# A causal convolution and a SwiGLU layer on one core: the second pair's tokens fetched by thirds, three of its sums moved

## The chip, the cores and the metric

The program runs on one core of a Trainium2 chip. Its engines are named as in the profile: PE multiplies matrices, DVE and POOL work on vectors, ACT evaluates functions, SP issues DMA transfers. The metric is the device time of one execution in microseconds. The kernel before took 2605.76 us, the median of four runs (2605.2 to 2605.84).

## The reference

The input `x` has 8 sequences of 4096 tokens with 192 channels. The first part is a causal convolution of seven taps: the 192 channels are eight heads of 24, each head has its own seven weights (a softmax over the taps), and a token is the weighted sum of itself and the six tokens before it. The second part works on all 32768 tokens: each is scaled by the inverse root of the mean of its squares, then

```
g   = xn @ w_gate        # 192 -> 1536
val = xn @ w_val         # 192 -> 1536
out = (silu(g) * val) @ w_out   # 1536 -> 192
```

Everything is float32.

## The kernel before, in words

The tokens are taken in 32 pairs of blocks: a pair is 1024 tokens, two halves g of T = 512. For each pair DVE, ACT and POOL make the convolution and the scaling (`yn`, heads on partitions), the heads are written to a scratch tensor `xd` of 192 channels by 1024 tokens in DRAM (`place`, L636, one transfer of 16 partitions for each head of 24 channels), and it is read back with the channels on partitions into `xb` (`fetch`, L649 for pair 1; `fetch_part`, L662, for the later pairs). `xb` is [128, 2, 3, 512]: the lower 64 partitions and the upper 64 hold the same tokens, the second index is the half g, the third the third k of the channels (64 channels each). `x_op(i)` names such pieces: 0 to 2 are the three thirds of half 0, 3 to 5 those of half 1, 6 to 15 are ten sums in `xc`.

Pair 0 goes through a plain path: `plain` multiplies by the weights (L1012), and `outer` multiplies by `w_out` (L1052) and sums the two row halves of each output bank (ACT copies one half, L1060; DVE adds the other, L1064; one store for each half of the tokens, L1069). From pair 1 on a product scheme is used that needs fewer multiplications, on combinations of the inputs: eleven token sums for a pair (`x_sum`, L671, listed in `XSUM`), combinations of the weights (`w_sums`, L346 and L350, made once by POOL) and of `w_out` (`out_sums`, L826, made once by POOL). PE's products for a pair (L760) run in the order of `CHAINS`; a product (v, i) goes into the bank of its sum v, once for the lower row half (h = 0) and once for the upper (h = 1). The chain of pair 1 begins with (4,11), (1,4), (5,6), (4,9), (0,8). Each product is two records in the trace.

The order of the work around the change is set by a list with a place for each action: `put(at, action)` enters it, `emit` gives it out by rising place. The outer stage starts at `base`, one of its 96 steps is 37.5 places, and `c` is `base + 200`. Each engine and each DMA queue executes its share in this order. While PE works through the outer products of pair 0, the list holds:

- on POOL the weight sums of the last two units (L350, L346), then for pair 2 the factor of the scaling (L478, L481, L484), one L826, the scaling itself (L499, which waits for the transpose L491 on DVE), and the eleven other L826;
- on SP the writes of heads 0, 2, 4, 6 of pair 1 (the odd heads are on ACT's queue), then `fetch(1)`, the store of pair 0's first half (L1069), pair 2's heads, the store of the second half, and loads of later tokens;
- on DVE taps of pair 2 (L445), L1064 for the first bank of pair 0, pair 2's reduction (L472, L473, L474), the first two token sums of pair 1, L1064 for the second bank (ps6), nine more sums, the transpose L491, L1064 for the third bank (ps7) and for the fourth (ps4). Then comes the work of pair 1.

PE's product (1,4) puts its upper half into bank ps7, and (5,6) into ps4, which the L1064 set free. The sums are given out in the order 0, 1, 7, 2, 3, 5, 6, 10, 8, 9, 4 of `XSUM`. Sum 0 reads the middle thirds of both halves, sum 1 the last third and sum 0's result. Product (4,11) reads what sum 6 writes, (1,4) what sum 10 writes, (5,6) the middle third of half 1 itself, (0,8) sum 8's result.

After pair 1 the order is written out by hand in `ORDER`, the same for each pair, and `fetch_part` reads the tokens by halves.

Of the kernel before, what the change touches and what calls it, by code (L numbers as in the profile page):

```python
# [19 lines left out]
def kernel(  # L20
# [22 lines left out]
    T = 512  # L43
# [3 lines left out]
    HP = P // 2  # L47
    KP = D // HP
# [188 lines left out]
    def load_out(i):  # L237
# [28 lines left out]
        out=taps[:], in0=w_sb[:], in1=stat[:].to_broadcast([P, H, K]), op=ALU.subtract  # L266
# [7 lines left out]
        out=taps[:], in0=taps[:], in1=ssum[:].to_broadcast([P, H, K]), op=ALU.mult  # L274
# [51 lines left out]
    xb = cst.tile([P, 2, KP, T], F32, name="xb")  # L326
# [315 lines left out]
    def fetch(p):  # L642

        if p >= PAIRS:
            return
        xd = scr.pop(p)
        for g in (1, 0):
            for rows in (LOW, UPP):
                nc.sync.dma_start(  # L649
                    out=xb[rows, g],  # L650
                    in_=xd[:, g * T : (g + 1) * T].rearrange("(k p) t -> p k t", p=HP),
                )

    mark = dram.tile([1, 2], F32, name="mark")
# [343 lines left out]
    def plain(hts):  # L998


        groups = [(u, g, f) for u in range(NU) for g in (1, 0) for f in range(NF)]
        groups[0 : 2 * NF] = [(0, g, f) for f in range(NF) for g in (1, 0)]
        held = {}

        def products():
            for u, g, f in groups:
                if len(hts) <= u:
                    hts.append(big.tile([P, 2, NF, T], F32, name="ht"))
                bks = held[u, g, f] = [free[h].pop(0) for h in range(2)]
                for k in range(KP):  # L1010
                    for h in range(2):
                        nc.tensor.matmul(  # L1012
                            out=bank(h, bks[h])[:], lhsT=wf[u][HALF[h], k * NF + f, :],
                            rhs=xb[HALF[h], g, k, :], start=(k == 0), stop=(k == KP - 1),
                            skip_group_check=True,
                        )
                yield

        def silus():
            for i in groups:  # L1020
                sg = tiles.pop(0)
                nc.scalar.activation(out=sg[:], in_=bank(0, held[i][0])[:], func=AF.Silu)
                held[i].append(sg)
                yield

        def values():
            for u, g, f in groups:
                *bks, sg = held.pop((u, g, f))
                nc.vector.tensor_tensor(  # L1029
                    out=hts[u][:, g, f, :], in0=bank(1, bks[1])[:], in1=sg[:], op=ALU.mult  # L1030
                )
                tiles.append(sg)
                for h in range(2):
                    free[h].append(bks[h])
                yield

        return products(), silus(), values()
# [117 lines left out]
    p, sl, v = plain(hts)  # L1155
# [25 lines left out]
    base = NU * SPAN  # L1181
    put(base - 1, lambda: outer(0, hts, base))
    put(base + 445, functools.partial(next, pieces["t"], None))
    put(base + 450, functools.partial(fetch, 1))
    both.extend(flat[:, i * T : (i + 1) * T] for i in range(NK - len(both)))
    rest.extend(t[:, 2, :] for t in tl6)
    put(base + 1317, lambda: tiles.extend(t[:, i, :] for t in tl6 for i in range(2)))
    c = base + 200
# [11 lines left out]
    later(norm(2), c + 1510, c + 1600, c + 2310, c + 2420, c + 2440)  # L1200
    later(place(2), c + 2450)
    xat = [c + i for i in (1660, 1730, 2060, 2130, 2200, 2270, 2290)]
    xat += [c + i for i in (2360, 2370, 2380, 2390)]
    for i, at in zip((0, 1, 7, 2, 3, 5, 6, 10, 8, 9, 4), xat):
        put(at, functools.partial(x_sum, i))
    later(out_sums(), *[base + 2600 + 60 * i for i in range(4 * NM)])
# [49 lines left out]
```

## Time and profile before

| what | value |
|---|---|
| median of four runs | 2605.76 us |
| the profiled execution | 2605.84 us |
| its span, first to last instruction | 2603.7 us |
| PE busy, share of the span | 2571.3 us, 99% |
| DVE, POOL, ACT | 2308.9 us (89%), 2188.5 us (84%), 1545.5 us (59%) |
| mean granted clock of PE | 0.998 |
| pair 0: plain products, outer products | 38.3 to 100.9 us, 101.0 to 134.3 us |
| heads of pair 1 written, fetch of pair 1 issued | from 112.6 us, 119.2 to 121.8 us |
| eleven sums of pair 1 on DVE | 129.8 to 137.8 us |
| first product of pair 1 | 135.40 us |

A line of a timeline has the start in us, the length, the engine, the line of the kernel, the operation, what it writes and reads, shapes and a count, and in brackets the idle time of the engine before it and what ended it. A group line has, behind the bar, busy time, mean ns of one, then the idle time before the group. Instructions that follow each other without a wait overlap by up to 0.1 us in the records, so the length of one is a little more than its share of the engine. PE's upper and lower row halves work at the same time.

### The profile page before, as it was taken

The numbers are of one execution on the slowest core, as the hardware profiler recorded it, in microseconds if no ns is written. First come the engines' busy times: TensorE is split into PE (matmuls) and PEld (weight loads), VectorE is DVE, ScalarE is ACT, GpSimd is POOL, SyncE is SP. The second block draws the span as 40 slices with busy tenths as digits, with TensorE's granted clock in tenths as the row PEclk, the third lists the DMA queues.
The fourth block names the chain that finished last, engine by engine and source line by source line (L and its number), as shares of the span: only waits on it lengthen the run. The fifth ranks groups of instructions, "written<-read, shape, count | busy, mean of one in ns | idle before, by whom it ended". The sixth has DMA issues, their size and how long they took to land.

```text
span 2603.7 us, 60625 instructions
## 1 busy us (share of the span) xinstructions
PE 2571.3 (99%) x23794; PEld 1766.3 (68%) x23794; DVE 2308.9 (89%) x3679; ACT 1545.5 (59%) x2812; POOL 2188.5 (84%) x1786
## 2 busy tenths in 40 slices
PE   6999999999999999999999999999999999999999
PEld 3776667666676667776676676666766666766666
DVE  8998989989989889889899898899898898988975
ACT  5375555765556765557655567655576555676554
POOL 3888889888898888898888898888988888988877
PEclk9999999999999999999999999999999999999999
DMA  6222331313322223312133222233222333122210
GB/s 144 51 51 45 63 61 39 58 33 63 63 51 44 45 51 63 63 39 56 32 63 64 51 44 45 50 63 63 41 53 38 58 63 56 40 54 41 50 44 13
DMA packets 512602, 137.35 MB, mean 53 GB/s; under 512 B 484284, under 2 KB 486844, under 8 KB 512189
## 3 DMA queue, kind: packets, MB, share of 16 engines
q1 hardware_dynamic: 509068, 132.80, 27.1%
q8 instruction: 186, 3.05, 0.5%
q10 hardware_dynamic: 3248, 0.69, 0.1%
q14 instruction: 100, 0.82, 0.1%
HBM read 83.87 MB, written 49.55 MB: 51 GB/s over the span
## 4 chain that ended last, share of the span: by engine, by line
PE 95%; DVE 2%; DMA 1%; issue 0%; ACT 0%; POOL 0%; SPq 0%; ACTq 0%; DVEq 0%; POOLq 0%
PE ps L760 62%; PE ps L900 33%; PE ps L1012 1%; DVE ht L1029 0%; DMA x<-in_x_dram 0%; DMA xb<-xd 0%; DVE xc L304 0%; DVE y L406 0%; DVE y L421 0%; DVE xc L671 0%; DVE y L394 0%; PE ps L595 0%; DVE wf L319 0%; ACT xb L615 0%; DMA xd<-yn 0%
## 5 line engine op out<-in xcount | busy, mean ns | idle before, releaser
L760 PE MATMUL ps<-xc,wf 64*128 64x512 f32 x4960 | 1217.6, 591 | 2.2 <-DVE xc L671 1.1
L760 PEld LDWEIGHTS ps<-xc,wf 64*128 64x128 f32 x4960 | 684.4, 186 | 375.7 <-issue 179.2
L760 PE MATMUL ps<-xb,wf 64*128 64x512 f32 x2480 | 683.1, 591 | 0.0
L709 ACT ACTIVATE tile<-ps 128x512 f32<-128x512 f32 x678 | 391.2, 593 | 391.1 <-PE ps L760 297.6
L709 ACT ACTIVATE tls<-ps 128x512 f32<-128x512 f32 (+1 forms) x562 | 323.3, 589 | 438.0 <-PE ps L760 221.3
L812 POOL TENSOR_TENSOR ht<-ht,tile 128x512 f32<-128x512 f32 x329 | 419.0, 1275 | 142.8 <-ACT tile L805 66.2
L760 PEld LDWEIGHTS ps<-xb,wf 64*128 64x128 f32 x2480 | 356.3, 187 | 180.5 <-issue 94.1
L812 POOL TENSOR_TENSOR ht<-ht,tls 128x512 f32<-128x512 f32 x260 | 330.6, 1274 | 85.9 <-ACT tls L805 42.5
L709 ACT ACTIVATE ps<-ps 128x512 f32<-128x512 f32 (+1 forms) x589 | 336.1, 580 | 89.1 <-PE ps L760 31.8
L928 POOL TENSOR_TENSOR early<-ht 128x512 f32<-128x512 f32 x279 | 354.9, 1277 | 4.9
L445 DVE SCALAR_TENSOR_TENSOR ps<-xh,tp,ps 128x512 f32<-128x512 f32 x450 | 320.2, 748 | 2.7 <-ACT ps L437 0.5
L900 PE MATMUL ps<-ht,wo_sb 128*32 128x128 f32 (+2 forms) x5208 | 318.6, 380 | 0.0
L900 PEld LDWEIGHTS ps<-ht,wo_sb 128*32 128x32 f32 x5208 | 234.1, 110 | 81.7 <-POOL ht L812 23.6
L900 PE MATMUL ps<-ht,x 128*32 128x128 f32 (+2 forms) x4464 | 250.7, 379 | 0.0
L792 DVE TENSOR_TENSOR tile<-ps,tile 128x512 f32<-128x512 f32 x349 | 237.4, 683 | 10.6 <-PE ps L760 5.6
L928 POOL TENSOR_TENSOR ht<-ht 128x512 f32<-128x512 f32 x186 | 238.9, 1285 | 4.9
L792 DVE TENSOR_TENSOR ht<-ps,tile 128x512 f32<-128x512 f32 x328 | 222.5, 680 | 6.2 <-ACT tile L709 6.2
L900 PEld LDWEIGHTS ps<-ht,x 128*32 128x32 f32 x4464 | 184.9, 110 | 60.8
L805 ACT ACTIVATE tile<-tile 128x512 f32<-128x512 f32 x349 | 214.5, 625 | 0.1
L792 DVE TENSOR_TENSOR ht<-ps,tls 128x512 f32<-128x512 f32 x292 | 198.9, 681 | 7.2 <-ACT tls L709 3.6
L792 DVE TENSOR_TENSOR tls<-ps,tls 128x512 f32<-128x512 f32 x271 | 184.8, 683 | 16.6 <-PE ps L760 13.4
L900 PE MATMUL ps<-early,x 128*32 128x256 f32 (+2 forms) x3348 | 196.0, 379 | 0.0
(130 smaller groups left out, 3249.2 us busy)
## 6 DMA issues: line engine op xcount, KB each, us to landing
xb<-xd SPq DMA_DIRECT2D x124, 384.0 KB
xd<-yn SPq DMA_DIRECT2D x244, 96.0 KB
xh<-in_x_dram SPq DMA_DIRECT2D x192, 105.0 KB
out_dram<-o_sb SPq DMA_DIRECT2D x122, 96.0 KB
out_dram<-o_sb SPq DMA_DIRECT2D x62, 128.0 KB
xh<-in_x_dram SPq DMA_DIRECT2D x56, 98.4 KB
out_dram<-o_sb SPq DMA_DIRECT2D x122, 32.0 KB
ht<-in_moe_w_gate_dram SPq DMA_DIRECT2D x12, 192.0 KB
```

Of the source, the lines that this page charges most:

```text
L445: nc.vector.scalar_tensor_tensor(out=dst, in0=xk, scalar=w, in1=at, op0=ALU.mult, op1=ALU.add)
L709: nc.scalar.activation(out=dst, in_=src, func=AF.Copy, scale=float(s))
L760: nc.tensor.matmul(out=self.new(v, h, True) if first else self.old(v, h), lhsT=wf[self.u][HALF[h], WAT[i], :], rhs=x_op(XOP[i])[HALF[h]], ...
L792: nc.vector.tensor_tensor(out=self.hv(v) if h else t[:], in0=self.old(v, h), in1=t[:], op=plus(s))
L805: nc.scalar.activation(out=t[:], in_=src[:], func=AF.Silu)
L812: engine[eng].tensor_tensor(out=self.hv(v), in0=src, in1=t[:], op=ALU.mult)
L900: nc.tensor.matmul(out=self.bank(b)[i * Q : (i + 1) * Q, at : at + n], lhsT=left, rhs=cols, start=fresh, stop=True, skip_group_check=True, ...
L928: engine[eng].tensor_tensor(out=dst, in0=a, in1=b, op=op)
L1012: nc.tensor.matmul(out=bank(h, bks[h])[:], lhsT=wf[u][HALF[h], k * NF + f, :], rhs=xb[HALF[h], g, k, :], start=(k == 0), stop=(k == KP - 1 ...
```

## The change

`fetch(1)` reads `xd` by the thirds of the channels in place of the halves of the tokens. There are six transfers where there were four; each covers 64 channels and all 1024 tokens, so that it depends on the writes of only those heads that its 64 channels touch (heads 0 to 2, 2 to 5, and 5 to 7). The bytes are the same. In the list, the places of the last three sums (8, 9 and 4) go from `c + 2370`, `2380`, `2390` to `base + 2895`, `2900`, `2905`, which is behind L491 and the L1064 of ps7 and ahead of the L1064 of ps4. The first eight sums keep their order. On PE and ACT the order of the instructions is as before; on POOL as well.

```diff
@@ fetch(p)
-        for g in (1, 0):
+        for k in range(KP):
             for rows in (LOW, UPP):
                 nc.sync.dma_start(
-                    out=xb[rows, g],
-                    in_=xd[:, g * T : (g + 1) * T].rearrange("(k p) t -> p k t", p=HP),
+                    out=xb[rows, :, k, :],
+                    in_=xd[k * HP : (k + 1) * HP, :].rearrange("p (g t) -> p g t", t=T),
                 )
@@ the list for pair 1
     xat = [c + i for i in (1660, 1730, 2060, 2130, 2200, 2270, 2290)]
-    xat += [c + i for i in (2360, 2370, 2380, 2390)]
+    xat += [c + 2360] + [base + i for i in (2895, 2900, 2905)]
     for i, at in zip((0, 1, 7, 2, 3, 5, 6, 10, 8, 9, 4), xat):
         put(at, functools.partial(x_sum, i))
```

## The prediction

> **What bounds the kernel now.** I read the page's busy table first, then the groups by line, then the chain of waits around the second pair's fetch (112 to 139 us), and there the timelines of PE, DVE and POOL.
>
> ```profile
> PE 2571.3 (99%) x23794; PEld 1766.3 (68%) x23794; DVE 2308.9 (89%) x3679; ACT 1545.5 (59%) x2812; POOL 2188.5 (84%) x1786
> ...
> L760 PE MATMUL ps<-xc,wf 64*128 64x512 f32 x4960 | 1217.6, 591 | 2.2 <-DVE xc L671 1.1
> ```
>
> PE is the bound. Of the large matmul groups (L760, L900) this one alone has idle time before it, 2.2 us in the whole run. PE's timeline shows that both pieces lie at the start of pair 1, which is what the edit touches:
>
> ```profile
> 135.40 1.95 PE L760 MATMUL ps<-xc,wf 64*128 64x512 f32 x6 [1.11 <-DVE xc L671]
> 138.44 0.69 PE L760 MATMUL ps<-xc,wf 64*128 64x512 f32 x1 [1.08 <-DVE o_sb L1064]
> ```
>
> Nothing later waits, so what the edit gains or loses here reaches the end unchanged, and the gain has a ceiling. PE's last outer matmul (L1052) ends at 134.29; three f32 products of two records each run at 0.43 us a record on each row half. The first product without a gap after it is the upper half of (5,6), in PE's order the third on that half. It starts at 139.40 in the records; without any wait it could start after two products, four records, at 134.35 + 4 x 0.43 = 136.1. So the edit can win 3.3 us at most. The chain of waits (start, length, what) says what holds it:
>
> ```profile
> 115.25 3.81 DMA xd<-yn
> ...
> 121.18 8.53 DMA xb<-xd
> ...
> 135.90 1.89 DVE xc L671 x3
> 137.78 0.15 DVE s L491
> 137.94 0.45 DVE o_sb L1064
> ```
>
> The heads land until 119.06, the fetch until 129.71, then eleven sums and the L1064 that frees bank ps7. The next rows to read are POOL's and DVE's in steady work, near 205 us, since the two share something:
>
> ```profile
> 204.68 1.74 POOL L928 TENSOR_TENSOR tls<-ht,nt 128x512 f32<-128x512 f32 x1
> ```
>
> ```profile
> 205.20 1.77 DVE L671 TENSOR_TENSOR xc<-xb 128x512 f32<-128x512 f32 x1
> ```
>
> And POOL's timeline at the place itself:
>
> ```profile
> 125.00 3.41 POOL L350 TENSOR_TENSOR wf<-wf 128x128 f32<-128x128 f32 x7
> 128.38 1.02 POOL L346 TENSOR_SCALAR wf<-wf 128x128 f32<-128x128 f32 x2
> 129.47 0.20 POOL L478 TENSOR_SCALAR r<-r 128x8 f32<-128x8 f32 x1
> 129.75 1.68 POOL L481 TENSOR_TENSOR r<-r,nhalf 128x8 f32<-128x8 f32 x1
> ...
> 138.07 2.87 POOL L499 TENSOR_TENSOR yn<-y,s 128x1536 f32<-128x1536 f32 x1 [4.69 <-ACT tile L709]
> ```
>
> A token sum (L671) takes 0.69 alone and 1.77 beside a POOL tensor_tensor, and POOL's op takes 1.74 where the page's mean for L928 is 1.28: they take turns, instruction by instruction. Beside L481 a sum keeps its 0.69, and an L1064, which reads PSUM, keeps 0.45 to 0.55 beside L499. Before the change the sums start at 129.83, when POOL has just finished its weight sums (129.40), and L499 waits for L491 (its wait ends at 137.98, 0.04 after L491), behind the last sum. So today they hardly meet.
>
> **The change, part by part.**
>
> *Issues on SP.* Four L649 of 0.60 to 0.64 us become six: two more, 0.5 us (an L659 costs 0.26) to 1.7 us (an L144 0.86); I take 1.3. They are hidden. By the landing records the heads arrive at 115.1, 115.6, 116.7, 117.1, 117.8, 118.1, 118.9 and 119.1. SP is free at 116.07, so the first third (heads 0 to 2) issues at 116.8, the second (to head 5) at 118.2, the third at 119.5 to 120.8. Next on SP is the L1069 store at 131.7, which waits for DVE.
>
> *Landing.* The same 1.57 MB. Before: issue 119.18, first packet 120.6, last landing 129.71, 9.1 us of flow. After: first packet about 118.3, last landing near 127.4, the second third near 124.7. Bounds: no gain (129.7), or 3 us.
>
> *The first sums move under POOL's weight sums.* DVE is free from 125.57 (L474). Sum 0 needs only the middle third and goes at once; sum 1 needs the last, about 127.6. From 125.41 POOL needs 4.26 us of its own to the end of L478 (129.67). Five sums get turns in it, 0.62 each: 3.1, so L478 ends at 132.8. L481 follows, 1.68, to 134.5; the two L484 (0.2 each) after sum 10's rest, to 135.05. DVE's eight sums are through by 134.7 (before: 135.98), so they win 1.3, not 2.3.
>
> *The three sums behind L1064.* New DVE order: sum 10, L491, L1064 (ps7), sums 8, 9, 4, L1064 (ps4). L491 waits for L484 and ends at 135.4, ps7 is free at 135.9. But L491 also releases POOL's L499, which starts about 135.65, after an L826, while DVE is in L1064. Sum 8 then stands behind L499: 135.65 + 2.87 = 138.5. After it sums and the eleven queued L826 take turns: 3 x 0.58 + 2 x 0.55 = 2.85, to 141.4, and L1064 0.53, to 141.9. The same reckoning puts the L1064 of before at 139.20, where the trace has 138.85, so I take 0.35 off: 141.55. The matmul follows 0.12 later, at 141.7 against 139.40: **+2.3 us**. PE's order is unchanged, so it stands at bank ps4 with only two and a half products done. Bounds: if POOL's chain kept its time (L499 from 132.9), -0.4; if a sum lost to L499 only the 1.1 us that the 1.77 row shows, 1.8 less, +0.5; if all eight sums took turns ahead of it and nothing is taken off, +3.9.
>
> What waits behind: L786 and the rest of DVE wait for PE as before, ACT too; POOL's next L812 at 148 has slack, since the L826 end near 146; the stores and loads on SP come 2 to 4 us later, and the next fetch is at 189.
>
> The Trainium skill has a rule for this (SBUF — State Buffer, "Who interferes with whom"): a VectorE instruction with two SBUF inputs and a GpSimd instruction that reads SBUF exclude each other for the whole instruction. The rows agree for 1.28 us instructions; none shows a sum against the 2.87 us of L499. By the rule the step costs the full +2.3 above; by the shortest reading of the row, the +0.5.
>
> *PE's clock.* The three sums open a silence on PE from about 137.0 (products (4,11), (1,4) and the lower half of (5,6) done) to 141.7, 4.7 us. PE's timeline has one like it, and the view by stretches (PE busy first, PEclk third from the end) shows the clock around it:
>
> ```profile
> 29.62 0.80 PE L595 MATMUL ps<-xc,y 128*128 128x128 f32 x2 [5.59 <-ACT xc L588]
> ```
>
> ```profile
> 20.00:30.00 10.00, 3.48 (x9) 1.25 (x7) 9.12 (x16) 7.68 (x23) 0.00 (x0) 0.84 1.17 178
> 30.00:40.00 10.00, 8.90 (x55) 7.98 (x56) 8.75 (x23) 8.16 (x17) 0.00 (x0) 0.82 0.23 25
> ...
> 134.00:138.00 4.00, 2.24 (x8) 0.70 (x6) 3.96 (x8) 1.08 (x2) 0.00 (x0) 1.00 0.00 0
> ```
>
> PEclk 0.84 and 0.82 over 10 us each are 3.2 + 3.6 = 6.8 us at half clock (26.83 to 33.66 in the clock records), 4.0 of them with work waiting: 2.0 us lost. Gaps of 1.1 us (134 to 138) left the clock at 1.00. A silence of 4.7 us is much nearer to 5.59: **+2.0 us**. Bounds: 0, and half of 6.8, 3.4.
>
> The skill (TensorE: Matmul & The Clock Gate, "What's actually happening") lets the clock fall after one idle window of about 3.4 us, free-running. A window of it that is wholly idle falls inside 4.7 us only about four times in ten (an estimate from that page), and then the sum would more often be +2.3 alone. The drop in the trace came 2.8 us after the last matmul, sooner than that.
>
> **Sum.** 2.3 + 2.0 = +4.3 on the profiled execution's own 2605.84 (span 2603.7 and 2.1 around it) is 2610.1; that execution is 0.08 above the median, so 2610.0.
>
> **Rivals.** *Slower without the clock drop:* +2.3, 2608.1. For it: the products just before the silence may keep the clock up, and whether it falls may hang on its phase. *As meant:* if L499 did not hold up sums 8, 9, 4 nor the weight sums the first ones, L1064 (ps4) ends near 135.3 and PE runs through: -3.3, 2602.5. Against it: the 1.77 rows. *Nearly even:* L499 early (133) or the sums passing it, -0.4 to +0.5, about 2605.8. *Past the bound:* the place is again L1064 (ps4); POOL's chain a further 0.6 late (+2.9) and the clock down from the resumption on for its longest, 3.4 of loss: +6.3, 2612.1. It decides once the loss of clock exceeds 2.9 on top of 2.3. That the change does not do what it says is excluded by the order of both programs: six L649 with waits on their own heads, three L671 moved.
>
> **How the numbers follow.** Chances: +4.3 case 0.48 (2608.2 to 2611.6), no clock drop 0.24 (2606.3 to 2609), even 0.10, as meant 0.10, past the bound 0.08. Leaving out the last two, the range is 2604.5 to 2611.6. A change under 0.2% (5.2 us) is what a measurement of this kernel can hardly tell from none: 2600.5 to 2611.0. Over it lie the last case and a fifth of the first: slower 0.17. Faster by more than 3.3 is excluded by the ceiling, but for surprises: 0.01. Same 0.82.
>
> **What would show it.** L671's first start at 125.6 to 126, in records over 1 us beside L350; L478 at 132 to 133; an L671 of over 2 us beside L499; the L1064 of ps4 ending near 141.5; PE idle over 4 us before (5,6), released by L1064; PEclk under 1.00 in 138 to 146. I am wrong if sum 8 runs 0.69 beside L499, if L499 starts before 134, or if PE's idle stays under 3 us.

## The result and the profile after

The changed kernel takes 2609.55 us, the median of 41 runs (2608.18 to 2611.42), against 2605.78 us for the kernel before in the same comparison (61 runs). The ratio is 1.0014, with a 95% interval of 1.001 to 1.0019: slower by 0.14%, 3.8 us, inside the 0.2% that was called no change, and on the slow side of it. The profiled execution took 2610.75 us, its span 2608.6.

On the page the idle time of PE's products has moved from one group to another, from 2.2 us in two pieces to 4.4 us in one:

```profile
PE 2575.3 (99%) x23794; PEld 1764.1 (68%) x23794; DVE 2315.6 (89%) x3679; ACT 1545.6 (59%) x2812; POOL 2191.4 (84%) x1786
...
L760 PE MATMUL ps<-xb,wf 64*128 64x512 f32 x2480 | 682.3, 591 | 4.4 <-DVE o_sb L1064 4.4
```

PE's timeline shows the place. PE as a whole now has no idle time up to the lower half of (5,6); only the upper half of (1,4) is held for about 0.4 us, to 136.05, by the L1064 of ps7, while other products run. The upper half of (5,6) stands for 4.38 us until L1064 has freed ps4. Such a stretch in which PE runs no matmul is called a silence here.

```profile
136.66 0.59 PE L760 MATMUL ps<-xb,wf 64*128 64x512 f32 x1
141.62 1.22 PE L760 MATMUL ps<-xb,wf 64*128 64x512 f32 x1 [4.38 <-DVE o_sb L1064]
141.63 1.22 PE L760 MATMUL ps<-xc,wf 64*128 64x512 f32 x1
142.64 1.06 PE L760 MATMUL ps<-xb,wf 64*128 64x512 f32 x1
```

What stands before that L1064 is in DVE's timeline. The first token sum starts at 126.18, 3.65 us earlier than before, and sum 10 ends at 133.04. Then DVE waits 2.26 us for POOL, and after L491 and the L1064 of ps7 the last three sums take 5.2 us:

```profile
126.18 0.93 DVE L671 TENSOR_TENSOR xc<-xb 128x512 f32<-128x512 f32 x1
...
132.35 0.69 DVE L671 TENSOR_TENSOR xc<-xc 128x512 f32<-128x512 f32 x1
135.31 0.25 DVE L491 STREAM_TRANSPOSE s<-s 128x64 f32<-128x64 f32 x1 [2.26 <-POOL s L484]
135.47 0.52 DVE L1064 TENSOR_TENSOR o_sb<-ps,o_sb 128x384 f32<-128x384 f32 x1
135.92 4.19 DVE L671 TENSOR_TENSOR xc<-xb 128x512 f32<-128x512 f32 x2
140.03 1.07 DVE L671 TENSOR_TENSOR xc<-xb,xc 128x512 f32<-128x512 f32 x1
141.03 0.54 DVE L1064 TENSOR_TENSOR o_sb<-ps,o_sb 128x384 f32<-128x384 f32 x1
```

The first line with two sums is sum 8 at 3.20 us and sum 9 at 1.07 in the single records. POOL's timeline beside it gives the reason for both waits, the late L484 and L499 from 135.78 to 138.60:

```profile
131.05 1.66 POOL L346 TENSOR_SCALAR wf<-wf 128x128 f32<-128x128 f32 x2
132.78 0.32 POOL L478 TENSOR_SCALAR r<-r 128x8 f32<-128x8 f32 x1
133.18 1.67 POOL L481 TENSOR_TENSOR r<-r,nhalf 128x8 f32<-128x8 f32 x1
134.92 0.35 POOL L484 COPY s<-r 128x32 f32<-128x32 f32 x2
135.23 0.59 POOL L826 TENSOR_TENSOR x<-wo_sb 128x192 f32<-128x192 f32 x1
135.78 2.82 POOL L499 TENSOR_TENSOR yn<-y,s 128x1536 f32<-128x1536 f32 x1
138.53 2.03 POOL L826 TENSOR_TENSOR x<-wo_sb 128x192 f32<-128x192 f32 x2
```

And the view by stretches (PE, PEld, DVE, ACT and POOL busy, then PEclk third from the end) shows PE's clock through the silence and behind it:

```profile
134.00:138.00 4.00, 3.25 (x16) 1.55 (x15) 2.69 (x3) 2.12 (x5) 3.94 (x5) 1.00 0.02 4
138.00:142.00 4.00, 0.38 (x2) 0.38 (x4) 4.00 (x5) 0.28 (x1) 4.00 (x5) 0.88 0.35 79
142.00:146.00 4.00, 4.00 (x10) 1.49 (x10) 1.42 (x3) 0.60 (x1) 3.91 (x8) 0.50 0.75 184
146.00:150.00 4.00, 4.00 (x18) 1.74 (x16) 2.84 (x6) 1.96 (x4) 0.00 (x0) 0.77 0.99 140
```

Before, it was 1.00 in all four stretches; the third of them was

```profile
142.00:146.00 4.00, 4.00 (x22) 3.07 (x20) 3.86 (x8) 2.17 (x4) 4.00 (x8) 1.00 0.64 143
```

The clock records of the changed kernel have it at half from 141.01 to 147.84. Record by record against the profile of before, PE is 0.67 us behind at the end of the outer products (a difference of the start-up, 134.96 against 134.29), 2.23 us at the upper half of (5,6), 5.27 us at 148 and 5.42 us by 180. From there it stays, apart from 0.4 us that come back in single steps further on; the spans differ by 4.9 us. So the whole effect, but for the start-up's part in this one execution, is made between 134 and 148 us: about 1.6 us of wait (2.23 less 0.67) and 3.1 us of half clock (the seven steps from 141.62 to 147.76 take 6.13 us, and at 0.43 would take 3.0).

### The profile page after: what moved, and what is told of

Read it like the earlier page. It is cut to its first block, busy times and chain, and to the rows that moved or that the text cites. A ratio compares the mean times of both kernels' runs of the same rounds, so it can differ in the third digit from the quotient of the medians.

```text
span 2608.6 us, 60632 instructions
## 1 busy us (share of the span) xinstructions
PE 2575.3 (99%) x23794; PEld 1764.1 (68%) x23794; DVE 2315.6 (89%) x3679; ACT 1545.6 (59%) x2812; POOL 2191.4 (84%) x1786
## 4 chain that ended last, share of the span: by engine, by line
PE 94%; DVE 2%; DMA 1%; SPq 1%; POOL 1%; issue 1%; DVEq 0%; POOLq 0%
PE ps L760 62%; PE ps L900 33%; POOL wf L350 1%; DMA xh<-in_x_dram 0%; DMA ht<-in_moe_w_val_dram 0%; SPq L217 0%; DVE ht L1029 0%; SPq L1149 0%; DMA x<-in_x_dram 0%; DVE y L421 0%; DVE wf L319 0%; DVE xc L304 0%; SPq L144 0%; DVE xc L671 0%; DVE xc L287 0%
```

## The experiments

The kernel before took 2605.58 us in the first group of four (33 runs) and 2605.69 us in the second of two (21 runs). Each experiment's own median is over 11 runs.

### The thirds alone

The changed fetch, with the three sums back at their old places:

```diff
-    xat += [c + 2360] + [base + i for i in (2895, 2900, 2905)]
+    xat += [c + i for i in (2360, 2370, 2380, 2390)]
```

> The fetch by thirds, with the three sums at their old places. My theory (sums 8, 9, 4 are held up by POOL's L499, and PE's silence costs clock): sum 10 still ends near 133.0, the last three follow at 0.6 each to 134.9 ahead of L491, so L499 cannot stand before them; L1064 (ps7) ends near 136.0, L1064 (ps4) near 136.5, the upper half of (5,6) starts near 136.9, some 3 us ahead of the kernel before; PEclk stays 1.00. Time near 2603.0, about 2.5 to 3 us under the kernel before. Rival (the six transfers, or sums under POOL's weight sums, are what costs): no better than before, 2606 or more.

Measured: 2602.39 us (2601.77 to 2603.47), ratio 0.9989, interval 0.998 to 0.9998: 3.2 us under the kernel before. DVE's timeline:

```profile
131.00 0.69 DVE L671 TENSOR_TENSOR xc<-xc 128x512 f32<-128x512 f32 x1
131.61 1.29 DVE L671 TENSOR_TENSOR xc<-xb 128x512 f32<-128x512 f32 x2
132.82 0.68 DVE L671 TENSOR_TENSOR xc<-xb,xc 128x512 f32<-128x512 f32 x1
134.28 0.24 DVE L491 STREAM_TRANSPOSE s<-s 128x64 f32<-128x64 f32 x1 [0.77 <-POOL s L484]
134.45 0.98 DVE L1064 TENSOR_TENSOR o_sb<-ps,o_sb 128x384 f32<-128x384 f32 x2
```

Sums 8, 9 and 4 fit into the time in which DVE would have waited for L484, and take 0.7 us each there. Both L1064 follow at once, and PE's idle at this place is 0.15 us:

```profile
135.02 0.69 PE L760 MATMUL ps<-xc,wf 64*128 64x512 f32 x1 [0.15 <-DVE o_sb L1064]
```

The rival, that six transfers or sums under the weight sums cost something that shows, falls. The fetch by thirds is a gain; by the interval it is between 0.5 and 5.2 us.

### The moved sums alone

The fetch of before, with the places of the change:

```diff
-    xat += [c + i for i in (2360, 2370, 2380, 2390)]
+    xat += [c + 2360] + [base + i for i in (2895, 2900, 2905)]
```

> The fetch by halves as before, with only the three sums moved. My theory: sum 10 ends at 136.0 and L491 at 136.1, L499 starts near 136.3 and holds sum 8 to 139.7; the L1064 of ps4 ends near 142.0 to 142.5 and PE is silent from 137.6 to 142.5; +3 us of wait and 0 to 3.4 us of clock, 2609 to 2612, likeliest 2610.5, so at least as slow as both parts together. Rival (the move as such is good, since ps7 comes free 2 us earlier): a gain of 0.4 us, 2605.4.

Measured: 2610.42 us (2609.71 to 2612.09), ratio 1.002, interval 1.0011 to 1.0028: 4.8 us over the kernel before. DVE's and PE's timelines have the same picture as the change, 1.5 us later:

```profile
136.87 0.24 DVE L491 STREAM_TRANSPOSE s<-s 128x64 f32<-128x64 f32 x1
137.03 0.52 DVE L1064 TENSOR_TENSOR o_sb<-ps,o_sb 128x384 f32<-128x384 f32 x1
137.47 4.10 DVE L671 TENSOR_TENSOR xc<-xb 128x512 f32<-128x512 f32 x2
```

```profile
138.16 1.02 PE L760 MATMUL ps<-xb,wf 64*128 64x512 f32 x2
143.09 1.22 PE L760 MATMUL ps<-xb,wf 64*128 64x512 f32 x1 [3.90 <-DVE o_sb L1064]
```

The clock falls here too, to half from 141.00 to 147.82 in the clock records. DVE does not wait for L484 at all, and L499, released by L491, still stands before sum 8, which takes 3.10 us. So L499's hold alone is enough for the loss. The two parts do not add up: -3.2 and +4.8 would make +1.6, and together they make +3.8. The timelines suggest why: in the change the first sum starts 4.62 us earlier than here (126.18 against 130.80) but L491 only 1.56 (135.31 against 136.87), since DVE then waits 2.26 us for L484, and the three sums at their old places, which would fill that wait, are gone. The difference of 2.2 us is taken from medians whose intervals are some 2 us wide each way, so its size is not certain.

### The scaling of pair 2 behind the sums

The changed kernel, with L491, L499 and the head writes that follow them put behind the L1064 of ps4:

```diff
-    later(norm(2), c + 1510, c + 1600, c + 2310, c + 2420, c + 2440)
-    later(place(2), c + 2450)
+    later(norm(2), c + 1510, c + 1600, c + 2310, base + 3795, base + 3796)
+    later(place(2), base + 3797)
```

> The changed kernel with L491, L499 and the writes of pair 2's heads put behind the L1064 of ps4. My theory: sums 8, 9 and 4 take about 0.7 us each, 133.5 to 135.4, the L1064 of ps4 ends near 136.0, the upper half of (5,6) starts near 136.5 and the clock stays 1.00: about 2602.3, 3.5 us under the kernel before and 7 under the changed one. Rival (the sums are slow for another reason, such as the fetch or PE's reads): they stay over 1 us each and the time over 2606.

Measured: 2601.75 us (2600.99 to 2603.05), ratio 0.9987, interval 0.9978 to 0.9995: 3.8 us under the kernel before and the fastest of all. DVE's timeline, where the same three sums stand at the same place between the two L1064:

```profile
132.21 0.55 DVE L1064 TENSOR_TENSOR o_sb<-ps,o_sb 128x384 f32<-128x384 f32 x1
132.68 1.28 DVE L671 TENSOR_TENSOR xc<-xb 128x512 f32<-128x512 f32 x2
133.88 0.69 DVE L671 TENSOR_TENSOR xc<-xb,xc 128x512 f32<-128x512 f32 x1
134.48 0.55 DVE L1064 TENSOR_TENSOR o_sb<-ps,o_sb 128x384 f32<-128x384 f32 x1
134.95 0.23 DVE L491 STREAM_TRANSPOSE s<-s 128x64 f32<-128x64 f32 x1
```

Without L499 beside them the two sums that took 4.19 us take 1.28. PE has no idle time before any product here. The edit takes away two things at once, L499's hold and the 2.26 us that DVE waits for L484; the moved sums alone, with the hold and without that wait, cost 4.8 us. Together the two runs show that the order of L491 and the sums, not the sums' place as such, is what the change pays for.

### PE kept busy in the silence

The changed kernel with spare matmuls on PE between (1,4) and (5,6). They read a weight tile and `wo_sb` and write the bank that (5,6) then starts afresh; no result changes. In this kernel's profile the line numbers are 1 higher up to the spare matmuls, which are L883, and 7 higher behind them (L1064 is L1071).

```diff
+    FILL = 5
...
                 for h in range(2):
+                    if self.p == 1 and (u, v, i, h) == (0, 5, 6, 0):
+                        for _ in range(FILL):
+                            nc.tensor.matmul(
+                                out=ps[0][:], lhsT=wf[0][:, 0, :],
+                                rhs=wo_sb[:, 0:3, :].rearrange("p f d -> p (f d)")[:, 0:T], start=True, stop=True, skip_group_check=True,
+                            )
                     self.units[u].product(h, v, i)
```

> The changed kernel with five spare 128x512 matmuls on PE between products (1,4) and (5,6), into the bank that (5,6) overwrites; 0.86 us each, 4.3 us, in the silence of 4.4 to 4.9 us. They change no result. My theory (PE's silence lowers its clock): the wait stays, the L1064 of ps4 ends near 141.5, PEclk stays 1.00 from 134 to 150, and the time falls by the clock's part, 1 to 3 us, to about 2608.0, +2.3 on the kernel before. Rival (the clock's drop is harmless, other engines bound PE then): no change, 2609.5.

Measured: 2606.9 us (2606.34 to 2608.14), ratio 1.0007, interval 0.9998 to 1.0016, which by itself can't be told from the kernel before. The work goes up by five matmuls and the time falls by 2.65 us against the changed kernel (2.45 when each is taken against its own kernel before, +3.77 and +1.32). PE's timeline shows the five in the gap, L1064 for ps4 ends at 140.29 as they do (not 141.5; the outer products ended 1.44 us earlier in this execution than in the change's), and the view by stretches shows the clock at 1.00 throughout:

```profile
135.81 4.56 PE L883 MATMUL ps<-wo_sb,wf 128*128 128x512 f32 x10
140.30 1.17 PE L761 MATMUL ps<-xb,wf 64*128 64x512 f32 x4
```

```profile
138.00:142.00 4.00, 4.00 (x14) 1.79 (x14) 2.76 (x4) 0.00 (x0) 4.00 (x7) 1.00 0.56 124
142.00:146.00 4.00, 4.00 (x21) 2.18 (x19) 3.90 (x8) 2.31 (x5) 2.65 (x5) 1.00 0.87 199
```

So of the 3.8 us that the change costs, about 2.5 are the clock after the silence and 1.3 the wait itself. All 11 executions with the spare matmuls (2606.34 to 2608.14) are faster than all 41 of the changed kernel (2608.18 to 2611.42), but the run's own interval goes from -0.5 to +4.2 us, so the split is an estimate. The profiles bear it out: counted from the end of the outer products to the end of the span, which leaves out the start-up, it is 2469.4 us before, 2473.6 in the change and 2471.0 here, +4.2 and +1.6.

### Two spare matmuls in place of five

```diff
-    FILL = 5
+    FILL = 2
```

> The changed kernel with two spare matmuls in PE's silence instead of five: 1.7 us of work, some 2.8 us of silence left. If the clock falls only after a silence near those seen to lower it (4.4 and 5.6 us), it stays 1.00 and the time is that with five, 2606.9. If 2.8 us are enough in some executions, it lies between 2606.9 and 2609.5; if always, at 2609.5.

Measured: 2607.09 us (2606.05 to 2607.97), ratio 1.0004, interval 0.9995 to 1.0013, the same as with five. What was left silent was less than expected, since the lower half of (5,6) follows the spare matmuls:

```profile
138.34 1.12 PE L761 MATMUL ps<-xb,wf 64*128 64x512 f32 x2
140.96 0.69 PE L761 MATMUL ps<-xb,wf 64*128 64x512 f32 x1 [1.49 <-DVE o_sb L1071]
```

PE as a whole was silent for 1.5 us, its upper half for 2.6, and PEclk was 1.00 in the stretches from 134 to 150. So the run does not try the 2.8 us that it was meant to try. Nor is the length of the silence what decides by itself: with the moved sums alone, the last matmul ended at 139.18 and the clock fell 1.82 us later, at 141.00 (see the last section).

### Both banks first

The changed kernel with the three sums behind both L1064:

```diff
-    xat += [c + 2360] + [base + i for i in (2895, 2900, 2905)]
+    xat += [c + 2360] + [base + i for i in (3795, 3796, 3797)]
```

> The changed kernel with sums 8, 9 and 4 put behind both L1064, so that ps4 comes free at once; L491 and L499 stay where the change has them, so L499 still stands ahead of sum 8. My theory (what cost was that PE's bank ps4 hung behind sums that hung behind L499): sum 8 is again over 3 us long, but PE goes through (5,6) and (4,9) and only (0,8) waits for sum 8, from about 138.6 to 139.2; the silence is under 1 us, PEclk stays 1.00, and the time is near 2603.6, 2 us under the kernel before. Rival (L499's hold alone costs it, whatever hangs behind): near 2609.

Measured: 2605.61 us (2604.57 to 2606.78), ratio 0.9999, interval 0.999 to 1.0008: as the kernel before, 3.9 us better than the change and 2 us worse than expected. PE's timeline has the expected wait at (0,8), 0.37 us, and a second one that was not expected; DVE's has what it waits for:

```profile
138.48 1.13 PE L760 MATMUL ps<-xc,wf 64*128 64x512 f32 x4 [0.37 <-DVE xc L671]
140.98 2.15 PE L760 MATMUL ps<-xc,wf 64*128 64x512 f32 x7 [1.37 <-DVE tile L786]
```

```profile
135.60 3.73 DVE L671 TENSOR_TENSOR xc<-xb 128x512 f32<-128x512 f32 x2
139.25 1.07 DVE L671 TENSOR_TENSOR xc<-xb,xc 128x512 f32<-128x512 f32 x1
140.25 1.28 DVE L786 TENSOR_TENSOR tile<-ps,tile 128x512 f32<-128x512 f32 x2
```

L499, over at 137.86, holds sum 8 here as well (2.73 us of the 3.73); sum 9, beside L826, takes 1.07. PE passes ps4, but L786, the first DVE work of pair 1, stands behind the sums on DVE, and PE needs it a few products on. What I left out was the queue behind the moved instructions. The theory that a hold by L499 costs what hangs behind it stands (2605.6, not 2609); the price I gave it was too low.

## Why the prediction was right, point by point

The forecast was 2610.0 us, no change that can be told and on the slow side; 2609.55 was measured, inside the range.

- *The issues and the landing.* The last third landed at 126.9 (forecast 127.4), the middle one at 124.7 (124.7). The step held, and it is what the thirds alone turn into 3.2 us, the forecast's ceiling of 3.3. The order with the scaling behind reached 3.8, which by its interval (1.3 to 5.7) does not show that the ceiling was too low.
- *The first sums under the weight sums.* L478 was forecast to end at 132.8 and ended at 133.10, or 132.4 without the 0.67 us of start-up. The sums themselves were costed too high: their records are 0.67 to 0.94 us beside L350 and L346 where the forecast had over 1 us, so sum 10 ended at 133.04 and not 134.7. It did not help, since L491 then waited 2.26 us for L484. The forecast sign "records over 1 us beside L350" was wrong.
- *The three sums behind L1064.* L499 started at 135.78 (forecast 135.65), before sum 8, which took 3.20 us; L1064 of ps4 ended at 141.57 (forecast 141.55). Without the start-up that is 140.9: the term of the sum was mis-sized, 2.3 us forecast and 1.6 found in the profiles (1.3 in the medians, by the kernel kept busy). About 0.5 of the difference is POOL's chain, which came through that much sooner than reckoned. For an instruction as long as L499 no row of before showed whether a sum stands behind it; sum 8's 3.20 us here against 0.68 in the kernel with the scaling behind shows that it does, as the rule of the Trainium skill has it (SBUF — State Buffer, "Who interferes with whom"). Beside L350 and L481 the sums' 0.67 to 0.94 us do not bear out that rule's exclusion for the whole instruction. The upper bound of +3.9 comes to about 4.5 by the prediction's own 0.62 us a sum (three more sums, and the 0.35 put back); nothing rests on it.
- *PE's clock.* It fell, as the likeliest case had it, 3.76 us after the last matmul's end and for 6.83 us. The term was mis-sized the other way: 2.0 forecast from the start-up's stretch, where 4.0 of 6.8 us had work waiting; here 6.2 had, so 3.1 in the profiled execution and about 2.5 in the medians. Going by the length of the silence was the weak step: in the records the clock changes at the ends of fixed steps of 3.41 us (last section). In the step before the fall, PE was busy for 0% of the time here (137.60 to 141.01), but for 18% in the start-up of before and for 47% with the moved sums alone. The Trainium skill (TensorE: Matmul & The Clock Gate, "What's actually happening") speaks of an idle, free-running window of about 3.4 us. The 3.41 us agree; that the window must be wholly idle, from which the prediction had its four times in ten, does not. Of the 41 executions none was under 2608.18, so none shows the 2.5 us that a run without the fall would gain.
- *The sum.* 1.3 + 2.5 = 3.8 in the medians for 2.3 + 2.0 = 4.3. Two terms were each off by half a microsecond or more, in opposite directions; that the sum came within 0.5 us is in part luck.
- *The rivals.* "As meant" failed at the move of the sums and was right for the thirds, which I had not priced by themselves. *Slower without the clock drop* fell with PEclk at 0.50 and with the 2.5 us that the spare matmuls won. The split of the change into two parts with opposite signs is the thing that the prediction did not say.

## What to carry to other kernels

An instruction that is moved behind another also moves behind everything that the other releases: L491 was 0.23 us of work on DVE, but it let loose a 2.82 us instruction on POOL beside which a moved sum took 3.20 us in place of 0.68. Cost the time at which the neighbour's long instruction starts, not only the places in one queue; where it can't be avoided, put the release behind the short work. And a silence on a matrix engine that is the bound can cost clock on top of the wait: 2.5 to 3.1 us after 4.38 us of silence in the change, and 2.4 after 3.90 with the moved sums alone (half of 143.09 to 147.82). Filling it with work that is thrown away bought 2.5 us here.

## What the runs showed that was not expected

- A DVE sum beside short POOL instructions loses little: in the changed kernel 0.67 to 0.94 us beside the 128-wide L350, for 0.69 alone, while most of the L350 beside them grow from 0.45 to between 0.78 and 0.98. Beside POOL's L481, 1.67 us on eight numbers a partition, a sum keeps its 0.69 (before, and with the thirds alone, where L481 itself takes 2.0). Whether that is because L481 reads so little, or because of its operation, was not tried.
- PE's clock changed on a grid. In each of the eight profiles the changes in the clock records lie whole multiples of 3.41 us apart; in the change they are at 28.37, 35.20, 141.01 and 147.84. Where the grid lies differs from execution to execution. Each fall before the end of the program stands at the end of a step in which PE, by its records, was busy for 47% of the time or less: 0% in the change, 18% at the start-up of before (23.42 to 26.83), 47% with the moved sums alone (137.58 to 141.00). With two spare matmuls the step from 139.34 to 142.75 was busy for 56%, and the clock stayed at 1.00. The share alone does not divide the cases, though: at the start-up of three kernels steps of 42 to 45%, of matmuls on all 128 rows, left it at 1.00.
- Each return to full clock stands at the end of the first step in which PE was busy for 94% or more. In the change the first step after the fall (141.01 to 144.43) was busy for 82% and the second for all of it, so the half clock lasted two steps, 6.83 us. At the start-up, with the same code, it lasted two steps in five of the profiles and one in the other three (29.58 to 33.00 with the scaling behind). So the price of a silence also hangs on where it falls on the grid, and that differs from execution to execution.
